# Splitting activations into even and odd halves, and moving side work, in a fused forward and backward kernel of two convolutions and a joint network

## The chip, the cores and the metric

The kernel runs on one core of one Trainium2 chip. The metric is device time in microseconds (us) of one execution. Times are medians of several executions; the span of a profiled execution is some 2 us shorter than its time; it runs from the first instruction to the last.

Engines: PE is TensorE's matmul, PEld its weight load, DVE is VectorE, ACT is ScalarE, POOL is GpSimd, SP is SyncE, which here only issues DMAs. A "q" after an engine means its sequencer, where DMAs are issued. In the code, matmuls write to tiles in PSUM, and copies take their results to SBUF, where `arena` is the kernel's own pool of memory.

## The reference, cut to what matters

```python
B, T, D, K, U = 2, 4000, 512, 15, 8
def _fwd_reference(x, w1, w2, g, w_f, w_g, w_o):
    xp = jnp.pad(x, ((0,0),(pad,pad),(0,0)))
    for i in range(K):  h = h + einsum("btc,cd->btd", xp[:, i:i+T, :], w1[i])
    h = gelu(h)[:, ::2, :]                       # every second row is kept
    ... the same with w2 on h gives f ...         # 1000 rows are left
    fe = einsum("btd,de->bte", f, w_f);  ge = einsum("bud,de->bue", g, w_g)
    j = tanh(fe[:, :, None, :] + ge[:, None, :, :])
    return einsum("btud,dv->btuv", j, w_o)
# the kernel returns this output and the gradients of all seven inputs for a given grad_out
```

All tensors are bf16. Because each convolution keeps every second row, a kernel that wants every second result reads its input with a step of two.

## The kernel before

The kernel has, in order of time: the first convolution, the second one, the joint network with its backward pass block by block, the backward pass of convolution 2 to its input (`acc_bP`, `acc_bQ`, `acc_bR`) and to its weights (`acc_k...`), and the same two for convolution 1. Each convolution is split so that three groups of accumulating matmuls, A, B and C (`acc_l..._0`, `_1`, `_2`), give two rows of results: `A + B` and `B - C`. Inputs are held by parity of the row (`par`), and also as differences of neighbours (`D`).

The forward loop, with the weight sums on POOL and the moving operand that steps by two:

```python
nc.gpsimd.tensor_tensor(WP[:, :, KT:KT + 4, :], WP[:, :, 0:13:4, :], WP[:, :, 2:15:4, :], op=ALU.add)      # L213
nc.gpsimd.tensor_tensor(WP[:, :, KT + 4:KT + 7, :], WP[:, :, 1:10:4, :], WP[:, :, 3:12:4, :], op=ALU.add)  # L214
for wi in range(nwin):
    r0 = wi * win                                        # win = 500
    accs = []
    for li, lst in enumerate(lists):                     # A, B, C
        acc = ps_pool.tile([P, 512], F32, tag="acc", name=f"acc_l{layer}_{li}")
        ...
                a0 = 2 * r0 + off
                nc.tensor.matmul(acc[:, :win], WP[:, cc, wi_, :],
                                 arr[an][:, cc, par, a0:a0 + 2 * win - 1:2], ...)
        accs.append(acc)
    nc.scalar.copy(bs, accs[1][:, :win])
    nc.vector.tensor_tensor(ye, accs[0][:, :win], bs, op=ALU.add)
    nc.vector.tensor_tensor(yo, bs, accs[2][:, :win], op=ALU.subtract)
    emit_out(b, dc, r0, win, ye, yo)                     # two epilogues and the stores
```

Only the B group uses the weight sums.

Start of the kernel: sixteen writes of halo zeros (the padding rows at both ends) to the hidden activations in DRAM are on the SP queue among the x loads.

```python
for b in range(B):
    for dc in range(NC):
        nc.sync.dma_start(HD[:, dc, :, b, 0:HALO], zt[:, :, 0:HALO])
        nc.sync.dma_start(HD[:, dc, :, b, HALO + T2:TH], zt[:, :, 0:HALO])
```

Joint stage: a gradient over 8 values of u is summed on PE with an identity matrix.

```python
pd = pw_f32("pdfe")
for u in range(U):
    nc.tensor.matmul(pd[:, :CH], ident[:], dpre[:, u, :], start=(u == 0), stop=(u == U - 1))
evac("act", DFET[:, ec, b, r0:r0 + CH], pd[:, :CH])
```

End of the joint stage: the w_g gradient leaves PSUM through staging buffers that are released at once, so that the next allocation takes the same place and has to wait for the output write.

```python
for dc in range(NC):
    pwg = pw_f32("pwg")
    nc.tensor.matmul(pwg[:, :D], Gnat[:, dc * P:(dc + 1) * P], DGEN, start=True, stop=True)
    stb, st = AR.new(BF16, [D])
    evac("act", st, pwg[:, :D])
    nc.sync.dma_start(out_6[dc * P:(dc + 1) * P, :], st)
    AR.release(stb)
```

Backward convolution: the order of three groups and the step of two.

```python
for nm in ("P", "Q", "R"):
    ...
        if an == "Y":
            f = 2 * n0 + ofs
            rhs = Y[:, dc, b, f:f + 2 * N + 1:2]
        else:
            rhs = S[:, dc, b, f:f + N + 1]               # always contiguous (all of Q)
        nc.tensor.matmul(acc[:, :N + 1], WT[:, dc, wi_, :], rhs, ...)
```

Last weight gradient: `comp_prep1(1)` starts the load of the even half of x (5.9 MB, on POOL) and then makes differences on VectorE (L1168 before, L1210 after), one for each batch element. One of these has to wait for the last `out_1` writes, whose source it overwrites.

```python
def comp_prep1(comp):
    if comp == 0: ...
    else:
        der["XHe"], der["xhe_blks"] = p5x_load(0, xhe_pre)      # gpsimd DMAs
    ...
    for b in range(B):
        xa, xb, xb2, xc, nr = der[(b, "ops")]
        nc.vector.tensor_tensor(der[(b, "P")], xa, xb, op=ALU.subtract)   # L1168
```

Of the kernel before, what the change touches and what calls it, by code (L numbers as in the profile page):

```python
# [17 lines left out]
P = 128  # L18
# [105 lines left out]
def build_kernel(ctx, tc, x, w1, w2, g, w_f, w_g, w_o, grad_out,  # L124
# [24 lines left out]
    make_identity(nc, ident[:])  # L149

# [22 lines left out]
    def gelu_epilogue(acc, n, tmp, h_out, g_out):  # L173
# [5 lines left out]
        nc.vector.tensor_tensor(h_out, s, acc, op=ALU.mult)  # L179
# [20 lines left out]
    def conv_fwd_k(layer, U_of, D_of, w_dram, n_half, win, emit_out, ps_pool, tmp, wp_blks, after_batch=None, cnt0=0,  # L200
# [4 lines left out]
        for b in range(B):  # L205
            arr = {"U": U_of(b), "D": D_of(b)}
            for dc in range(NC):
# [7 lines left out]
                for wi in range(nwin):  # L215
                    r0 = wi * win
                    accs = []
                    for li, lst in enumerate(lists):
                        acc = ps_pool.tile([P, 512], F32, tag="acc", name=f"acc_l{layer}_{li}")
                        k = 0  # L220
                        nk = NC * len(lst)
                        for cc in range(NC):
                            for (an, par, off, wi_) in lst:
                                a0 = 2 * r0 + off
                                nc.tensor.matmul(acc[:, :win], WP[:, cc, wi_, :],  # L225
                                                 arr[an][:, cc, par, a0:a0 + 2 * win - 1:2],
                                                 start=(k == 0), stop=(k == nk - 1))
                                k += 1
                        accs.append(acc)
# [27 lines left out]
    if "p1" in phases:  # L257
        with ExitStack() as es:
# [17 lines left out]

            for b in range(B):
                nc.gpsimd.memset(XTs[b][:, :, :, 0:HALO], 0.0)
                nc.gpsimd.memset(XTs[b][:, :, :, HALO + T1:TX], 0.0)
            zt = tmp1["hst"]  # L280
            nc.gpsimd.memset(zt[:, :, 0:HALO], 0.0)
            for b in range(B):
                for dc in range(NC):
                    nc.sync.dma_start(HD[:, dc, :, b, 0:HALO], zt[:, :, 0:HALO])
                    nc.sync.dma_start(HD[:, dc, :, b, HALO + T2:TH], zt[:, :, 0:HALO])
# [3 lines left out]
            def prep_x(b):  # L289
                cnt = prep_cnt[0]  # L290
                xb = x[b].rearrange("(blk p par) c -> par p blk c", p=CH, par=2)
                for par in range(2):
                    for gi in range(ngrp):
                        XN = AR.view(xn_blks[cnt % 2], BF16, [gsz, D], parts=CH)
                        dma(nc.sync, XN, xb[par][:, gi * gsz:(gi + 1) * gsz, :])
                        for cc in range(NC):
                            pt = ps_tp.tile([P, 1024], BF16, tag="tp", name="tp_x")
                            for kk in range(gsz):
                                nc.tensor.transpose(pt[:, kk * P:kk * P + CH],
                                                    XN[:, kk, cc * P:(cc + 1) * P], ident[:CH, :CH])  # L300
                            evac("dve" if cc % 2 == 0 else "act",
                                 XTs[b][:, cc, par, HALO + gi * gsz * CH:HALO + (gi + 1) * gsz * CH]
                                 .rearrange("p (k c) -> p k c", c=CH),
                                 pt.rearrange("p (k c) -> p k c", c=P)[:, :gsz, :CH])
                        cnt += 1
                hx = (TX - 1) // 2
                for (k0, k1) in ((0, hx), (hx, TX - 1)):
                    for cc in range(NC):
                        nc.vector.tensor_tensor(DXs[b][:, cc, :, k0:k1], XTs[b][:, cc, :, k0:k1],
                                                XTs[b][:, cc, :, k0 + 1:k1 + 1], op=ALU.subtract)  # L310
# [4 lines left out]
            def emit_out1(b, dc, r0, n, ye, yo):  # L315
                hst, gst = tmp1["hst"], tmp1["gst"]
                gelu_epilogue(ye, n, tmp1, hst[:, 0, :], gst[:, 0:2 * n:2])
                gelu_epilogue(yo, n, tmp1, hst[:, 1, :], gst[:, 1:2 * n:2])
                nc.sync.dma_start(HD[:, dc, :, b, HALO + r0:HALO + r0 + n], hst)
# [4 lines left out]
            def p2_load(b):  # L324
# [8 lines left out]
                for cc in range(NC):  # L333
                    nc.vector.tensor_tensor(dv[:, cc, :, 0:TH - 1], v[:, cc, :, 0:TH - 1], v[:, cc, :, 1:TH],
# [8 lines left out]
            def mid1(b, dc):  # L343
                if b == 0 and dc == 0:
# [13 lines left out]
    def p3_pre(pw_f32, pw_bf16):  # L358
        nc.gpsimd.memset(DFPT[:, :, :, 0:HALO], 0.0)
        nc.gpsimd.memset(DFPT[:, :, :, HALO + T2:TH], 0.0)  # L360
# [121 lines left out]
    def kbwd_accumulate(ps_pool, WT, Y, S, b, n0, N, comp):  # L482
        L = kbwd_lists()
        res = {}
        for nm in ("P", "Q", "R"):
# [4 lines left out]
            for (an, ofs, wi_) in lst:  # L490
                for dc in range(NC):
                    if an == "Y":
                        f = 2 * n0 + ofs
                        rhs = Y[:, dc, b, f:f + 2 * N + 1:2]
# [8 lines left out]
    def p4_setup(pool=None, tag="tp"):  # L503
        blk, DHPT = AR.new(BF16, [NC, B, TX])
        p4_state["DHPT_blk"], p4_state["DHPT"] = blk, DHPT
        nc.gpsimd.memset(DHPT[:, :, :, 0:HALO], 0.0)
        nc.gpsimd.memset(DHPT[:, :, :, HALO + T1:TX], 0.0)
# [71 lines left out]
    if "p3" in phases:  # L579
        with ExitStack() as es:  # L580
# [39 lines left out]
            DPRE = [AR.new(BF16, [U, CH]) for _ in range(NBUF)]  # L620
            JN = [AR.new(BF16, [U, D], parts=CH) for _ in range(NBUF)]
            OST = [AR.new(BF16, [U, D], parts=CH) for _ in range(NBUF)]
            loop_blks = [t[0] for lst in (FE, JT, OMJ, SQT, DO, DOT, DPRE, JN, OST) for t in lst]
# [67 lines left out]
            def emit_dj(k, ecs):  # L691
                b, rr, r0 = sbinfo(k)
                omj, dot = OMJ[k % NBUF][1], DOT[k % NBUF][1]
                for ec in ecs:
# [13 lines left out]
                    pd = pw_f32("pdfe")  # L708
                    for u in range(U):
                        nc.tensor.matmul(pd[:, :CH], ident[:], dpre[:, u, :], start=(u == 0), stop=(u == U - 1))  # L710
                    evac("act", DFET[:, ec, b, r0:r0 + CH], pd[:, :CH])
# [8 lines left out]
            def emit_batch_end(b):  # L720
                g2blk, G2T = AR.new(BF16, [NC, T2])
                nc.sync.dma_start(G2T, G2D[b])
                for dc in range(NC):
                    for wi in range(T2 // W2N):
                        s0 = wi * W2N
                        pf = pw_f32("pdf")
                        for ec in range(NC):
                            nc.tensor.matmul(pf[:, :W2N], WFT[:, ec, dc * P:(dc + 1) * P], DFET[:, ec, b, s0:s0 + W2N],
                                             start=(ec == 0), stop=(ec == NC - 1))
                        nc.vector.tensor_tensor(DFPT[:, dc, b, HALO + s0:HALO + s0 + W2N], pf[:, :W2N],  # L730
                                                G2T[:, dc, s0:s0 + W2N], op=ALU.mult)
# [27 lines left out]
            if "p4" in phases:  # L759
                blk, SQ2 = AR.new(BF16, [NC, B, T2 // 2 + 4])  # L760
                SQ2_st["blk"], SQ2_st["v"] = blk, SQ2
                k = 0
                for b in range(B):
                    for dc in range(NC):
                        eng = nc.vector if k % 2 == 0 else nc.gpsimd
                        eng.tensor_tensor(SQ2[:, dc, b, :], DFPT[:, dc, b, 0:TH - 1:2], DFPT[:, dc, b, 1:TH:2],
# [491 lines left out]
```

## Time and profile before

| | before |
|---|---|
| median time | 2190.79 us (4 runs, 2189.94 to 2193.62) |
| span of the profiled run | 2186.3 us |
| PE busy | 2061.4 us, 94% |
| PE idle inside its span (from the gaps between matmuls) | 113.3 us |
| half clock granted to PE (from the clock records) | 68.3 us, PE busy in 27.7 us of them |

PE is the limit, so two things count: how long each matmul occupies PE, and where PE idles. An idle gap of a few us can also bring a stretch at half clock that outlasts it. The Trainium skill (TensorE: Matmul & The Clock Gate, "Part 1: The HAM clock gate") describes this with windows of about 3.4 us; the trace agrees, its half-clock stretches are 3.41, 6.83, 10.24, 13.65 and 30.7 us long.

The groups of PE instructions of the kernel before, shapes kept apart. The columns are line, engine, operation, output and input, shapes and count, then busy us and the mean ns of one, then the idle time of PE just before them and who ended it.

```profile
L225 PE MATMUL acc_l<-arena 128*128 128x500 bf16 x2208 | 497.8, 386 | 3.5 <-POOL arena L213 2.3 <-POOL arena L214 0.9 <-DMA arena<-in_w_dram 0.3
L498 PE MATMUL acc_bP<-arena 128*128 128x501 bf16 x768 | 183.9, 383 | 0.7 <-ACT arena L166 0.7
L498 PE MATMUL acc_bQ<-arena 128*128 128x501 bf16 x768 | 174.1, 375 | 0.0
```

The mean of one runs from issue to the modelled end, and successive matmuls overlap, so it is not what one costs. The cost is the time from one start to the next, which I took from the trace at full clock: 222 ns for `acc_l`, `acc_bP` and `acc_bR` (median), 212 for `acc_bQ`, 210 for `pj`. The mean of `acc_l` is 223.6. The means above show the same difference: 386 and 383 for the operands with a step, 375 for `acc_bQ`, which is contiguous.

The waits of PE in the kernel before (engine, what waited, for what; total us, times, longest):

```profile
PE acc_kP L843 <- DVE arena L1168: 22.6, 1, 22.6
...
PE tp_dfp L930 <- ACT arena L166: 14.1, 3, 12.6
...
PE tpdo L666 <- DMA arena<-in_grad_out_dram: 8.3, 1, 8.3
PE tp_dx L1116 <- DVE arena L1066: 7.7, 3, 3.8
...
PE pge L416 <- DVE arena L168: 1.5, 1, 1.5
...
PE pdf L728 <- DVE arena L730: 1.2, 1, 1.2
```

Not shown are, among others, 17.6 us in four waits for the x loads. The largest of the list, in order of time (start, duration, engine, line, operation; in brackets the idle time before it and who ended it). Several other instructions lie between these lines.

```profile
1837.84 1.36 POOL L544 DMA_DIRECT2D arena<-in_x_dram  x1
...
1843.76 0.62 SPq L159 DMA_DIRECT2D out_dram<-arena  x1
...
1862.96 3.09 DVE L1168 TENSOR_TENSOR arena<-arena 125x5632 bf16<-125x5632 bf16 x1 [18.69 <-DMA out_dram<-arena]
1866.11 2.31 PE L843 MATMUL acc_kP<-arena 125*128 125x512 bf16 x5 [22.57 <-DVE arena L1168]
```

Read it backwards. PE waits for the VectorE subtraction, which waits for the out_dram writes issued from 1843.76 on. That wait ends at 1862.96 only, 19.2 us after the first of these writes was issued, with the 5.9 MB x load under way, which was issued just before them, from 1837.84 on.

### The profile page before, as it was taken

How to read it: one execution, taken by the hardware profiler on the slowest of the kernel's cores; microseconds unless marked ns; L12 is line 12 of the kernel's file. 1: busy time of each engine (PE TensorE's matmuls, PEld its weight loads, DVE VectorE, ACT ScalarE, POOL GpSimd, SP SyncE). 2: the span in 40 equal slices, each digit the busy share in tenths (PEclk: the TensorE clock that was granted, in tenths of full speed). 3: DMA queues.
4: the chain of work that ended last, by engine and by line, in shares of the span. 5: the costliest groups of instructions: out<-in, count | busy, mean ns of one | idle time of the engine just before them, and what ended most of it. 6: DMA issues, size and time to landing. Idle time of an engine off the chain costs nothing.

```text
span 2186.3 us, 29569 instructions
## 1 busy us (share of the span) xinstructions
PE 2061.4 (94%) x12032; PEld 1050.7 (48%) x12032; DVE 847.4 (39%) x1970; ACT 570.4 (26%) x1143; POOL 484.5 (22%) x424
## 2 busy tenths in 40 slices
PE   5999999999899999999799998899999996899999
PEld 3444444444566656666444444444445443344444
DVE  2554433543555555556364533432322232111310
ACT  1322122121655545552311233311212331000000
POOL 1332322353544444453020010130100001000000
PEclk9999999999999999999899999999999998899999
DMA  9423424653222222224310022134210104100000
GB/s 176 102 65 82 112 65 109 154 108 66 90 76 76 77 77 76 76 76 139 132 37 1 20 92 73 51 104 83 59 26 20 29 19 101 45 27 26 25 25 25
DMA packets 227408, 154.14 MB, mean 71 GB/s; under 512 B 167728, under 2 KB 219348, under 8 KB 223016
## 3 DMA queue, kind: packets, MB, share of 16 engines
q1 hardware_dynamic: 203592, 119.99, 21.0%
q10 hardware_dynamic: 19392, 20.49, 3.3%
q0 software_dynamic: 4288, 11.78, 2.5%
q8 instruction: 94, 1.54, 0.3%
q14 instruction: 42, 0.34, 0.1%
HBM read 100.02 MB, written 52.17 MB: 70 GB/s over the span
## 4 chain that ended last, share of the span: by engine, by line
PE 45%; ACT 3%; DVE 2%; DMA 1%; issue 1%; ACTq 0%; POOL 0%; DVEq 0%
PE acc_bP L498 7%; PE acc_bQ L498 7%; PE acc_kP L843 7%; PE acc_kR L843 7%; PE acc_bR L498 6%; PE acc_kQ L843 6%; ACT arena L166 2%; PE acc_k L866 2%; PE tp_wk L476 1%; DMA out_dram<-arena 1%; PE tp_dx L1116 1%; PE tp_hnk L1007 1%; DVE arena L168 0%; PE tp_dhp L1083 0%; DVE arena L1064 0%
## 5 line engine op out<-in xcount | busy, mean ns | idle before, releaser
L225 PE MATMUL acc_l<-arena 128*128 128x500 bf16 x2208 | 497.8, 386 | 3.5 <-POOL arena L213 2.3
L225 PEld LDWEIGHTS <-arena 128*128 128x128 bf16 x2208 | 212.8, 97 | 283.1 <-issue 5.8
L498 PEld LDWEIGHTS <-arena 128*128 128x128 bf16 x2208 | 211.4, 97 | 253.5 <-issue 1.0
L843 PEld LDWEIGHTS <-arena 125*128 125x128 bf16 x2016 | 196.6, 98 | 255.9 <-DVE arena L1168 22.8
L498 PE MATMUL acc_bP<-arena 128*128 128x501 bf16 x768 | 183.9, 383 | 0.7 <-ACT arena L166 0.7
L843 PE MATMUL acc_kP<-arena 125*128 125x512 bf16 x672 | 158.1, 383 | 22.6 <-DVE arena L1168 22.6
L658 POOL TENSOR_TENSOR arena<-arena 128x500 f32<-128x500 bf16 x128 | 130.4, 1019 | 202.7 <-ACT arena L650 202.6
L498 PE MATMUL acc_bQ<-arena 128*128 128x501 bf16 x768 | 174.1, 375 | 0.0
L650 ACT ACTIVATE arena<-arena 128x125 bf16<-128x125 f32 x512 | 158.7, 398 | 55.2 <-DVE arena L168 55.2
L498 PE MATMUL acc_bR<-arena 128*128 128x501 bf16 x672 | 158.6, 384 | 0.0
L843 PE MATMUL acc_kQ<-arena 125*128 125x512 bf16 x672 | 156.5, 379 | 0.0
L704 DVE SCALAR_TENSOR_TENSOR arena<-arena,pj 128x125 bf16<-128x125 bf16 x512 | 111.7, 282 | 112.6 <-PE pj L699 112.4
L843 PE MATMUL acc_kR<-arena 125*128 125x512 bf16 x672 | 155.0, 379 | 0.0
L717 PE MATMUL gwo<-arena 125*128 125x512 bf16 x512 | 141.6, 379 | 0.0
L848 ACT COPY arena<-acc_kQ 128x512 f32<-128x512 f32 x56 | 32.8, 586 | 399.3 <-PE acc_kQ L843 383.3
L850 DVE TENSOR_TENSOR arena<-acc_kP,arena 128x512 bf16<-128x512 f32 x56 | 38.7, 691 | 222.9 <-PE acc_kP L843 219.3
L699 PE MATMUL pj<-arena 128*128 128x500 bf16 x512 | 118.4, 373 | 5.4 <-ACT arena L166 5.3
L181 POOL TENSOR_TENSOR arena<-arena 128x500 f32<-128x500 f32 x48 | 63.1, 1315 | 241.8 <-ACT arena L178 230.9
L675 PE MATMUL po<-arena 128*125 128x512 bf16 x512 | 113.3, 379 | 0.0
L1064 DVE TENSOR_TENSOR arena<-arena 128x500 bf16<-128x500 f32 x32 | 23.8, 745 | 202.5 <-ACT arena L1062 202.5
L213 POOL TENSOR_TENSOR arena<-arena 128x2048 bf16<-128x2048 bf16 x16 | 65.4, 4088 | 116.0 <-DMA arena<-in_w_dram 116.0
L232 DVE TENSOR_TENSOR arena<-acc_l,arena 128x500 f32<-128x500 f32 x24 | 16.3, 678 | 190.1 <-ACT arena L231 190.1
(136 smaller groups left out, 2187.4 us busy)
## 6 DMA issues: line engine op xcount, KB each, us to landing
arena<-in_w_dram SPq DMA_DIRECT2D x64, 480.0 KB
out_dram<-arena SPq DMA_DIRECT2D x132, 128.0 KB
arena<-in_w_dram SPq DMA_DIRECT2D x8, 1920.0 KB
arena<-in_grad_out_dram SPq DMA_DIRECT2D x16, 896.0 KB
out_dram<-arena ACTq DMA_DIRECT2D x16, 896.0 KB
arena<-in_x_dram POOLq DMA_DIRECT2D x4, 2576.0 KB, 23.1
arena<-in_x_dram SPq DMA_DIRECT2D x8, 896.0 KB
arena<-HD SPq DMA_DIRECT2D x2, 2016.0 KB
```

The source lines that it names most:

```text
L166: nc.scalar.copy(out_ap, in_ap)
L181: nc.gpsimd.tensor_tensor(xsq, sm, z, op=ALU.mult)
L213: nc.gpsimd.tensor_tensor(WP[:, :, KT:KT + 4, :], WP[:, :, 0:13:4, :], WP[:, :, 2:15:4, :], op=ALU.add)
L225: nc.tensor.matmul(acc[:, :win], WP[:, cc, wi_, :], arr[an][:, cc, par, a0:a0 + 2 * win - 1:2], start=(k == 0), stop=(k == nk - 1))
L498: nc.tensor.matmul(acc[:, :N + 1], WT[:, dc, wi_, :], rhs, start=(k == 0), stop=(k == nk - 1))
L650: nc.scalar.activation(jt[:, ec, u, :], fe[:, ec, :], ACT.Tanh, bias=GE[:, ec, b * U + u:b * U + u + 1])
L658: nc.gpsimd.tensor_tensor(sq, jt[:, :, u, :], jt[:, :, u, :], op=ALU.mult)
L675: nc.tensor.matmul(po[:CH, :D], jt[:, ec, u, :], WO[:, ec, :], start=(ec == 0), stop=(ec == NC - 1))
L699: nc.tensor.matmul(pj[:, :4 * CH], WOT[:, vc, ec * P:(ec + 1) * P], dot[:, vc, 4 * uh:4 * uh + 4, :].rearrange("p u r -> p (u r)"), start= ...
L704: nc.vector.scalar_tensor_tensor(dpre[:, u, :], omj[:, ec, u, :], 1.0, pj[:, ul * CH:(ul + 1) * CH], op0=ALU.mult, op1=ALU.mult, accum_out ...
L717: nc.tensor.matmul(GWO[ec][:, :D], jn[:, u, ec * P:(ec + 1) * P], do[:, u, :], start=(k == 0 and u == 0), stop=(k == nsb_tot - 1 and u == ...
L843: nc.tensor.matmul(acc[:, :D], data(b, comp, kind, l + m, cc), dy(b, dk, l), start=(k == 0), stop=(k == nk - 1))
```

## The change

The intent: (1) hold each activation as an even and an odd half, so that a step of two becomes contiguous; (2) take a quarter of the `pdfe` sums from PE to VectorE; (3) start sooner, with the halo writes later and the groups in the order A, C, B, because only B needs the weight sums; (4) in the last stage hold the x load back behind a subtraction, by a tiny POOL copy into its target (the gate); (5) backward groups in the order P, R, Q, so that less is left after the last group; (6) smaller de-interleaving copies shared by ACT and VectorE. Core of the diff; the rest follows the new layout.

```diff
-                    accs = []
-                    for li, lst in enumerate(lists):
+                    accs = [None, None, None]
+                    for li in (0, 2, 1):
+                        lst = lists[li]
...
                                 a0 = 2 * r0 + off
+                                m0 = (a0 % 2) * (arr[an].shape[-1] // 2) + a0 // 2
                                 nc.tensor.matmul(acc[:, :win], WP[:, cc, wi_, :],
-                                                 arr[an][:, cc, par, a0:a0 + 2 * win - 1:2],
+                                                 arr[an][:, cc, par, m0:m0 + win],
...
-            for b in range(B):
-                for dc in range(NC):
-                    nc.sync.dma_start(HD[:, dc, :, b, 0:HALO], zt[:, :, 0:HALO])
-                    nc.sync.dma_start(HD[:, dc, :, b, HALO + T2:TH], zt[:, :, 0:HALO])
+            def halo_zeros():
+                HDz = HD.rearrange("p c r b t -> p (c r b) t")
+                nc.sync.dma_start(HDz[:, :, 0:HALO // 2], zt[:, :, 0:HALO // 2])
+                nc.sync.dma_start(HDz[:, :, HH - HALO // 2:HH + HALO // 2], zt)
+                nc.sync.dma_start(HDz[:, :, TH - HALO // 2:TH], zt[:, :, 0:HALO // 2])
...
             def mid1(b, dc):
+                if b == 0 and dc == 1:
+                    halo_zeros()
...
-        for nm in ("P", "Q", "R"):
+        for nm in ("P", "R", "Q"):
...
-                        rhs = Y[:, dc, b, f:f + 2 * N + 1:2]
+                        m0 = (f % 2) * (Y.shape[-1] // 2) + f // 2
+                        rhs = Y[:, dc, b, m0:m0 + N + 1]
...
+                    if ec % 4 == 3 and U == 8:
+                        tr = TRS[k % NBUF][1]
+                        df = dpre.rearrange("p u r -> p (u r)")
+                        nc.vector.tensor_tensor(tr[:, 0:4 * CH], df[:, 0:4 * CH], df[:, 4 * CH:8 * CH], op=ALU.add)
+                        nc.vector.tensor_tensor(tr[:, 4 * CH:6 * CH], tr[:, 0:2 * CH], tr[:, 2 * CH:4 * CH], op=ALU.add)
+                        nc.vector.tensor_tensor(DFET[:, ec, b, r0:r0 + CH], tr[:, 4 * CH:5 * CH], tr[:, 5 * CH:6 * CH],
+                                                op=ALU.add)
+                    else:
...
-                else:
-                    der["XHe"], der["xhe_blks"] = p5x_load(0, xhe_pre)
...
                     nc.vector.tensor_tensor(der[(b, "P")], xa, xb, op=ALU.subtract)
+                if comp == 1:
+                    for b in range(B):
+                        nc.gpsimd.tensor_copy(AR.view(xhe_pre[b], BF16, [L1 + 7, D], parts=CH)[:, 0, 0:1],
+                                              der[(B - 1, "P")][:, 0, 0:1])
+                    der["XHe"], der["xhe_blks"] = p5x_load(0, xhe_pre)
```

## The prediction

> **What bounds the kernel.** TensorE. The page gives PE 94% of 2186 us, DVE 39%, ACT 26%, POOL 22%; the table by stage shows PE busy 322 of 325 us in the first convolution, 165 of 165 in the second, 439 of 444 in the joint stage, 317 of 320 in the last weight gradient. Starts of successive matmuls (trace, full clock) separate two rates. The Trainium skill (TensorE: Matmul & The Clock Gate, Back-to-back issue gap) gives N/2.4 + 2.5 ns: 211 for N=500. `pj` (500 contiguous columns) takes 210 and `acc_bQ` (501 contiguous, at odd and even offsets) 212: they agree. But `acc_l`, `acc_bP` and `acc_bR`, whose moving operand steps by two bf16, take 222 (`acc_l` mean 223.6). The skill (SBUF — State Buffer, note on cachelines) would have that stride free, with several hits per 16-byte line; the trace says about 11 ns each.
>
> **What the change does.**
> 1. It stores each activation as an even and an odd half, so these operands become contiguous: 2208 `acc_l` matmuls save about 12 ns (-26 us), 1440 `acc_bP`/`acc_bR` save 10 ns (-14 us). All on PE, which is critical in those stages.
> 2. A quarter of the `pdfe` identity-matmul sums (128 of 512, about 58 ns each) go to three VectorE adds per block. DVE is half idle there: -6 us.
> 3. Start: sixteen tiny halo writes sat on the SP queue between the halves of the second x load (issued 1.8 and 15.5 us); PE waited 6.1 us for it. They move later. The order A, C, B needs POOL's weight sums last: the waits of 2.3 and 0.9 us and the half-clock window at 44.5 to 51.3 us should go. Together -10 us.
> 4. Last stage: PE idles 22.6 us before the first `acc_kP`, for a DVE subtraction that waits for out_dram writes, which land late among the x load issued on POOL just before (DMA 90% busy, mostly the software queue). The load now waits for that subtraction: the writes should land in 2 to 4 us (estimate), leaving about 9 us idle: -13 us.
> 5. P, R, Q order: after the last group of a pass only one DVE operation is left instead of an ACT copy and three; the `tp_dx` waits of 2.0, 1.8, 3.8 us shrink: -5 us.
> 6. De-interleaving copies are halved and shared by ACT (2.0 us per 1008 elements now) and DVE; derivative writes step 2 instead of 4 (1.5 to 1.6 us each now). Mostly hidden: -3 us.
> 7. Added: four HD writes per window instead of one, two half-size multiplies instead of one at each batch end, SQ2 on DVE alone. About +2 us.
>
> The 12.6 us idle before `tp_dfp` (PSUM held by the last `pwg` copies, whose staging waits for output writes) and the 8.3 us before `tpdo` should stay.
>
> **Prediction.** Sum -75 us: 2116 us, range 2098 to 2134. Faster by over 2%: 0.95; within 2%: 0.05; slower: 0.00.
>
> **What would show it.** Start-to-start of `acc_l`, `acc_bP`, `acc_bR` at 210 to 213 ns; first convolution matmul about 5 us earlier, no POOL wait; idle before `acc_kP` near 9 us; joint stage about 7 us shorter, nothing new waiting for the VectorE sums.
>
> **What would make it wrong.** The extra 11 ns may not come from the stride; the epilogue, serial through single buffers, may not keep up with faster windows; the thousands of 4 and 8 byte halo writes may delay weight loads; out_dram writes may land late for another reason.

## More of the kernel before

The epilogue of one half window ends with a POOL multiply and a VectorE operation with two SBUF inputs (L182 before, L187 after), here called the last epilogue step:

```python
def gelu_epilogue(acc, n, tmp, h_out, g_out):
    ...
    nc.gpsimd.tensor_tensor(xsq, sm, z, op=ALU.mult)
    nc.vector.scalar_tensor_tensor(g_out, xsq, 1.0, s, op0=ALU.add, op1=ALU.mult)     # L182
```

## The result, and the profile after

| | before | after |
|---|---|---|
| median time | 2190.65 us (12 runs, 2189.32 to 2194.03) | 2128.91 us (8 runs, 2124.36 to 2137.27) |
| ratio of the fast runs | | 0.9718, 95% interval 0.9705 to 0.973 |
| span of the profiled run | 2186.3 us | 2122.6 us |
| PE busy / idle inside its span | 2061.4 / 113.3 us | 2023.3 / 87.7 us |
| half clock, and PE busy in it | 68.3, 27.7 us | 64.9, 38.0 us |

A ratio is the mean time of one kernel's fast runs over that of the other's in the same rounds, so it is not quite the ratio of the medians. Executions over 1.5% slower than the fastest of the same kernel are left out of the means. The change is faster by 2.8%, inside the predicted range, but it saves 62 us where 75 were predicted. The sections that follow ask where the 13 us went. The runs of the changed kernel also spread over 13 us, those of the kernel before over 5; the profiled one is the fastest of the eight.

The stages tell more than the sum. Each is the time from one event on PE to the next, read from the trace. The two columns on the right belong to experiments that are told below.

| stage, from the event above to this one | before | after | difference | sums on VectorE | all edits |
|---|---|---|---|---|---|
| first `acc_l` (from the start) | 33.2 | 28.6 | -4.6 | 28.8 | 28.6 |
| last transpose of x | 74.3 | 71.3 | -3.0 | 70.4 | 61.8 |
| first `tpw` (rest of convolution 1) | 272.9 | 259.8 | -13.2 | 259.8 | 259.8 |
| first `acc_l` of convolution 2 | 6.0 | 13.8 | **+7.8** | 10.0 | 10.0 |
| first `pfe` (convolution 2) | 165.8 | 160.4 | -5.4 | 160.2 | 160.0 |
| first `po` | 14.3 | 7.6 | -6.8 | 7.6 | 7.6 |
| first `pdf` of batch element 2 (joint stage) | 443.7 | 435.4 | -8.4 | 435.1 | 435.0 |
| first `tpf` | 14.4 | 17.8 | **+3.5** | 14.4 | 14.6 |
| first `acc_bP` | 44.0 | 44.4 | +0.4 | 45.8 | 32.2 |
| first `tp_hnk` | 185.3 | 180.5 | -4.8 | 179.9 | 182.1 |
| first `acc_bP` of convolution 1 | 211.3 | 212.5 | **+1.2** | 208.9 | 209.2 |
| first `tp_dhp` | 275.3 | 266.5 | -8.8 | 262.5 | 262.7 |
| first `acc_kQ` of the last stage | 93.7 | 93.1 | -0.6 | 93.1 | 93.0 |
| first `acc_kP` of the last stage | 32.0 | 11.6 | -20.4 | 11.6 | 11.6 |
| end of the span | 320.2 | 319.4 | -0.8 | 319.2 | 319.3 |

The groups of PE instructions after, as before:

```profile
L232 PE MATMUL acc_l<-arena 128*128 128x500 bf16 x2208 | 473.3, 376 | 0.9 <-DVE arena L323 0.9
L522 PE MATMUL acc_bP<-arena 128*128 128x501 bf16 x768 | 179.6, 378 | 0.7 <-ACT arena L167 0.7
```

From start to start `acc_l` now takes 211 ns, `acc_bP` and `acc_bR` 212. The rates are those predicted, and the wait for POOL's weight sums before `acc_l` is gone.

The waits of PE after:

```profile
PE tp_dfp L968 <- ACT arena L167: 14.1, 1, 14.1
PE pge L439 <- DVE arena L169: 8.7, 1, 8.7
PE acc_kP L876 <- DVE arena L1210: 7.0, 1, 7.0
...
PE tp_hnk L1047 <- DVE arena L169: 4.5, 2, 3.8
...
PE pdf L762 <- DVE arena L739: 3.7, 1, 3.7
```

The wait before `acc_kP` fell from 22.6 to 7.0 us, and that for `grad_out` before `tpdo` is gone, which I had said would stay. Three waits are new or much longer: `pge` 1.5 to 8.7, `pdf` 1.2 to 3.7, `tp_hnk` with a longest of 3.8. All three wait for VectorE. VectorE in order of time in the changed kernel, at the end of convolution 1 and before the last `pdf` group:

```profile
363.00 0.71 DVE L187 SCALAR_TENSOR_TENSOR arena<-arena 128x500 bf16<-128x500 f32 x1 [0.80 <-POOL arena L186]
...
367.71 4.54 DVE L187 SCALAR_TENSOR_TENSOR arena<-arena 128x500 bf16<-128x500 f32 x1 [0.80 <-POOL arena L186]
...
978.44 3.84 DVE L739 TENSOR_TENSOR arena<-arena 128x125 bf16<-128x125 f32 x1
```

POOL at the same times:

```profile
367.64 4.04 POOL L218 TENSOR_TENSOR arena<-arena 128x2048 bf16<-128x2048 bf16 x1
...
978.09 4.05 POOL L487 TENSOR_TENSOR arena<-arena 128x2048 bf16<-128x2048 bf16 x1 [3.16 <-PE pdf L762]
```

The same VectorE operation takes 0.71 us once and 4.54 us the next time. The second time it began 0.07 us after a POOL weight sum and ended 0.6 us after it. The copies that PE needs for `pge`, 0.9 us of work, stand behind it in VectorE's queue. The other two waits look the same. L739, the last VectorE add of a sum, takes 3.84 us (median 0.28) beside the weight sum L487. A copy before `tp_hnk` takes 4.30 us beside the next one:

```profile
1227.87 4.05 POOL L487 TENSOR_TENSOR arena<-arena 128x2048 bf16<-128x2048 bf16 x1 [7.28 <-DMA arena<-in_w_dram]
1227.89 4.30 DVE L169 COPY arena<-arena 128x504 bf16<-128x504 bf16 x1 [1.43 <-PE tp_hnk L1047]
```

That suggested a theory, which the experiments below test: VectorE stands still while such a sum runs on POOL.

The last stage after, in order of time:

```profile
1797.86 0.30 POOL L1213 COPY arena<-arena 125x1 bf16<-125x1 bf16 x2 [5.29 <-DVE arena L1210]
...
1798.66 1.38 POOL L569 DMA_DIRECT2D arena<-in_x_dram  x1
...
1800.02 3.09 DVE L1210 TENSOR_TENSOR arena<-arena 125x5632 bf16<-125x5632 bf16 x1 [1.63 <-DMA out_dram<-arena]
```

The gate copy (POOL L1213) was released by the first subtraction (1794.71 to 1797.79), which waits for no write. It is the second one, at 1800.02, that waits for the writes. So the load was not held behind that one, as I had predicted; it started 1.4 us before it. But the first writes had been issued at 1796.60, ahead of the load, and PE went on with `acc_kP` at 1803.17.

### The profile page after: what moved, and what is told of

Its sections match the earlier page's. It is cut to its first block, busy times and chain, and to the rows that moved or that the text cites. A ratio compares the mean times of both kernels' runs of the same rounds, so it can differ in the third digit from the quotient of the medians.

```text
span 2122.6 us, 29361 instructions
## 1 busy us (share of the span) xinstructions
PE 2023.3 (95%) x11904; PEld 1052.9 (50%) x11904; DVE 878.3 (41%) x2062; ACT 558.0 (26%) x1143; POOL 482.6 (23%) x430
## 4 chain that ended last, share of the span: by engine, by line
PE 85%; ACT 8%; DVE 3%; DMA 2%; issue 1%; ACTq 0%; POOL 0%; SPq 0%; DVEq 0%; POOLq 0%
PE acc_l L232 22%; PE acc_bP L522 7%; PE acc_bQ L522 7%; PE acc_kP L876 7%; PE acc_kR L876 7%; PE acc_kQ L876 7%; PE acc_bR L522 6%; PE pj L725 5%; PE gwo L751 5%; ACT arena L167 4%; ACT arena L676 3%; PE acc_k L899 2%; PE tp_wk L499 2%; PE po L701 1%; PE tpdo L692 1%
## 5 line engine op out<-in xcount | busy, mean ns | idle before, releaser
L232 PE MATMUL acc_l<-arena 128*128 128x500 bf16 x2208 | 473.3, 376 | 0.9 <-DVE arena L323 0.9
L232 PEld LDWEIGHTS <-arena 128*128 128x128 bf16 x2208 | 215.5, 98 | 252.9 <-issue 5.4
L522 PEld LDWEIGHTS <-arena 128*128 128x128 bf16 x2208 | 213.6, 98 | 239.0 <-issue 2.5
L522 PE MATMUL acc_bP<-arena 128*128 128x501 bf16 x768 | 179.6, 378 | 0.7 <-ACT arena L167 0.7
L522 PE MATMUL acc_bR<-arena 128*128 128x501 bf16 x672 | 153.9, 376 | 0.0
L751 PE MATMUL gwo<-arena 125*128 125x512 bf16 x512 | 137.1, 379 | 0.0
L187 DVE SCALAR_TENSOR_TENSOR arena<-arena 128x500 bf16<-128x500 f32 x48 | 78.5, 1634 | 53.1 <-POOL arena L186 53.1
L487 POOL TENSOR_TENSOR arena<-arena 128x2048 bf16<-128x2048 bf16 x8 | 33.3, 4164 | 254.4 <-DMA arena<-in_w_dram 200.0
```

Source lines behind the costliest of these rows:

```text
L232: nc.tensor.matmul(acc[:, :win], WP[:, cc, wi_, :], arr[an][:, cc, par, m0:m0 + win], start=(k == 0), stop=(k == nk - 1))
L522: nc.tensor.matmul(acc[:, :N + 1], WT[:, dc, wi_, :], rhs, start=(k == 0), stop=(k == nk - 1))
L751: nc.tensor.matmul(GWO[ec][:, :D], jn[:, u, ec * P:(ec + 1) * P], do[:, u, :], start=(k == 0 and u == 0), stop=(k == nsb_tot - 1 and u == ...
```

## The experiments

Twelve kernels ran. The changed kernel did not run beside them; differences are taken to its median of 2128.91 us, and the kernel before had medians of 2190.6 to 2192.0 us.

### The layout alone

The kernel before with only the operand's step taken away, nothing stored differently. It reads wrong elements; shapes, waits and counts are those of before.

```diff
-                                                 arr[an][:, cc, par, a0:a0 + 2 * win - 1:2],
+                                                 arr[an][:, cc, par, a0:a0 + win],
...
-                        rhs = Y[:, dc, b, f:f + 2 * N + 1:2]
+                        rhs = Y[:, dc, b, f:f + N + 1]
```

> The kernel before, with only the step of the moving operand taken away in the forward and backward convolutions (the same start, columns next to each other, so results are wrong on purpose; nothing else moves). Theory, the step of two costs the 11 ns: starts of acc_l, acc_bP and acc_bR fall from 222 to 211 or 212 ns, and the time falls by 2208 x 12 + 1440 x 10 = 41 us, to about 2150 us, without any change of layout. Rival, the 11 ns belong to these matmuls for another reason (weights, accumulation): they stay at 222 ns and the time stays at 2190 us.

Measured: 2159.17 us, ratio 0.9851 (0.9831 to 0.9871), so 31 us of median and 27.3 us of span. The start-to-start times fell to 211 and 212 ns. Without the waits in it the mean of `acc_l` fell from 222.2 to 211.4 ns, so multiplied by the counts the rates alone would give 38 us (2208 × 10.8 + 1440 × 10.1 ns); the 41 us expected took the waits for a part of the rate. Most of the rest is found on PE: it idles 3.5 us more (116.8), and its busy time at half clock rose from 27.7 to 40.5 us; half of these 12.8 us, 6.4 us, is lost. My reading, which no run tests, is that the side chains were not made faster, so a faster PE meets them sooner, and short waits tip it into half-clock stretches. The mechanism holds; the gain on the clock is about three quarters of the product.

### What a step costs

The changed kernel, with convolution 1 reading its operand in steps of 1, 2, 4 and 8 for its four output blocks. Its output is wrong, which doesn't matter for the time.

```diff
+                                rhs = arr[an][:, cc, par, m0:m0 + win]
+                                if layer == 1:
+                                    sp = (1, 2, 4, 8)[dc]
+                                    rhs = arr["U"][:, cc].rearrange("p r t -> p (r t)")[:, off:off + sp * (win - 1) + 1:sp]
```

> The changed kernel, with the moving operand of the first convolution read at steps of 1, 2, 4 and 8 elements for the four output blocks dc 0 to 3 (wrong results on purpose). Theory, [...]211 ns at step 1, 222 at step 2, and clearly more at 4 and again at 8[...]. Rival, any step other than 1 costs a fixed 11 ns: 222 at 2, 4 and 8.

Measured (a single look, of unknown state; start to start at full clock): 211, 222, 442 and 879 ns. The cost is not a fixed 11 ns. From a step of 2 on it follows the span of memory that the 500 elements of one partition cover: 2000 bytes in 222 ns, 4000 in 442, 8000 in 879, which is 9.0 to 9.1 bytes per ns each time. At that rate the 1000 bytes of step 1 would take 111 ns (an estimate from these numbers), well under the 211 measured. The figure for a step of 8 rests on seven pairs at full clock. In most of those blocks PE was granted half the clock (163.8 and 177.5 us in one piece) although its matmuls followed each other without a gap, and there they also started 879 ns apart (median of 358 pairs). At this step the clock did not set the pace. A step of two lies just beyond the break-even point: 222 against 211. This is why the change gains only 5% on these matmuls. The Trainium skill (SBUF — State Buffer, "Door 1: The DMA port swizzle", note on cachelines) would have bf16 stride free up to 8; for a matmul's moving operand the measurement contradicts it.

### The gate

The changed kernel with the x load back where it was.

```diff
+                else:
+                    der["XHe"], der["xhe_blks"] = p5x_load(0, xhe_pre)
...
-                if comp == 1:
-                    for b in range(B):
-                        nc.gpsimd.tensor_copy(...der[(B - 1, "P")][:, 0, 0:1])
-                    der["XHe"], der["xhe_blks"] = p5x_load(0, xhe_pre)
```

> The changed kernel with the x load of the last stage put back where it was (issued before the subtraction, without the POOL copies that hold it back). Theory: out_dram writes again land late behind the load, PE again idles about 22 us before the first acc_kP instead of 7, and the time rises by 15 to 20 us. Rival, the shorter idle comes from the P, R, Q order (the last transposes start sooner): the idle stays under 10 us and the time within 3 us.

Measured: 2148.52 us, ratio 0.9805 (0.9787 to 0.9823), 20 us above the changed kernel; in its trace the stage before `acc_kP` is 15.6 us longer. The idle before `acc_kP` is back at 22.6 us; the load was issued from 1797.9 on, the writes from 1806.3 on, and they landed at 1825.3. The gate is needed.

### The order P, Q, R

The changed kernel with the backward groups in the old order.

```diff
-        for nm in ("P", "R", "Q"):
+        for nm in ("P", "Q", "R"):
```

> The changed kernel with the backward groups in the old order P, Q, R. Theory: the waits of tp_dx at the ends of passes return (0.2 us in the changed kernel's last pass, 1.8 to 3.8 us before) and the idle before acc_kP is about the same: 3 to 6 us slower. Rival, the order matters little: within 2 us.

Measured: 2144.79 us, ratio 0.9788 (0.9772 to 0.9804): 16 us above the changed kernel, not a few. The gate is still there, and the idle before `acc_kP` is 22.3 us all the same. Its last stage in order of time:

```profile
1802.36 3.08 DVE L1210 TENSOR_TENSOR arena<-arena 125x5632 bf16<-125x5632 bf16 x1
1805.37 0.67 DVE L1106 TENSOR_TENSOR arena<-acc_bQ,arena 128x500 bf16<-128x500 f32 x1
...
1806.61 1.39 POOL L569 DMA_DIRECT2D arena<-in_x_dram  x1
...
1807.84 0.61 SPq L160 DMA_DIRECT2D out_dram<-arena  x1
...
1826.37 3.09 DVE L1210 TENSOR_TENSOR arena<-arena 125x5632 bf16<-125x5632 bf16 x1 [18.41 <-DMA out_dram<-arena]
```

In this order the first subtraction comes before L1106, the last operation that the out_1 writes need. So the gate opens before the writes are issued, and the load goes ahead of them by 1.2 us. In the changed kernel L1106 comes before the first subtraction. The gain of the last stage therefore came from gate and order together; each alone gives nothing there.

### The order P, Q, R with the gate on both batch elements

If only the place of the load counts, a gate on both subtractions must bring the gain back without the new order.

```diff
-                        nc.gpsimd.tensor_copy(AR.view(xhe_pre[b], ...)[:, 0, 0:1],
-                                              der[(B - 1, "P")][:, 0, 0:1])
+                        for b2 in range(B):
+                            nc.gpsimd.tensor_copy(AR.view(xhe_pre[b], ...)[:, 0, b2:b2 + 1],
+                                                  der[(b2, "P")][:, 0, 0:1])
```

(and the order as in the run before)

> The changed kernel with P, Q, R in the backward pass (as the earlier run that lost 16 us) and the gate on the subtractions of both batches, so that the x load is issued after the one that waits for the out_dram writes. Theory (the order mattered through the place of the load against those writes): the idle before the first acc_kP falls from 22.3 to 8 to 10 us, and the time is about 13 us below the run with P, Q, R and the single gate: 2131. Rival (the order P, Q, R costs by itself, by the longer tail after the last pass): idle stays above 18 us and the time at 2142 to 2147.

Measured: 2121.87 us, ratio 0.9692 (0.9671 to 0.9712), 23 us below the run before. The idle is 7.1 us:

```profile
1795.22 3.09 DVE L1210 TENSOR_TENSOR arena<-arena 125x5632 bf16<-125x5632 bf16 x1 [3.17 <-DMA out_dram<-arena]
1798.37 1.89 PE L876 MATMUL acc_kP<-arena 125*128 125x512 bf16 x4 [7.05 <-DVE arena L1210]
...
1798.95 1.37 POOL L569 DMA_DIRECT2D arena<-in_x_dram  x1 [0.26 <-POOL arena L1214]
```

The wait for the writes ends 3.5 us after the first of them was issued (at 1791.73), as in the changed kernel (3.4 us), where it took 18.5 us in the run before, 19.0 without the gate and 19.2 in the kernel before. The load starts afterwards, when nothing waits for it. This settles the cause of the idle time. I had expected 13 us of gain; 23 came. The two profiled runs are even 30.6 us apart. Of these, 15.0 are the last stage; 8.3 are the transposes of x in the first stage (79.5 against 71.2 us) and 6.5 the stage of `tp_hnk`. The code is the same in these two, so they vary from run to run; why is said at the end of the account below.

This run is also no slower than the changed kernel with its P, R, Q. By stage, P, R, Q gains 3.4 us in the backward pass of convolution 1 and 4.3 before `acc_kP`, and loses 3.9 us up to the first `tp_hnk` and 1.5 between the first `tp_dhp` and the last stage (both runs with P, Q, R agree within 0.3 us on the three of these that the gate does not touch). At `tp_hnk` the cause shows in the trace: the copies on ACT and VectorE (L167, L169) that feed it are released by the last `acc_bQ` matmul, and in the new order that one comes a group later. Order P, R, Q helps one tail and hurts another; about 2 us are left.

### The sums on PE again

The changed kernel with all `pdfe` sums on PE.

```diff
-                    if ec % 4 == 3 and U == 8:
+                    if ec % 4 == 5 and U == 8:
```

> The changed kernel with every pdfe sum back on TensorE (no VectorE sums). Theory: the two stretches of the joint stage, 215.7 and 219.6 us in the changed kernel, grow by about 3.5 us each (64 matmuls of 58 ns), while the 3.7 us wait of pdf for the last VectorE add (3.84 us instead of 0.5, as POOL's weight sum runs beside it) goes away with its half-clock window: net 1 to 5 us slower, so near 2131 us. Rival, VectorE's extra work also slows the blocks: the stage does not grow, and the time falls by some 4 us.

Measured: 2136.5 us (2130.23 to 2145.25), ratio 0.9754 (0.9726 to 0.9783), 8 us above the changed kernel, where 1 to 5 were expected. Its runs overlap those of the changed kernel; the stages say more. The two halves of the joint stage are 5.7 and 5.9 us longer, more than the 3.7 each that 64 matmuls of 58 ns give. The rest is a wait: `pj` waits 5.0 us in total (13 times) for ACT's copies out of PSUM, 0.2 us in the changed kernel. Each sum on VectorE also saves ACT a copy. The wait before the last `pdf` group (the product of the summed gradient with w_f) gave 3.3 us back. So the item is worth 8 us net, and the wait that it adds comes from its last add, L739: 3.84 us instead of the median 0.28, beside POOL's weight sum L487.

### The forward order A, B, C

The changed kernel with the forward groups in the old order.

```diff
-                    for li in (0, 2, 1):
+                    for li in (0, 1, 2):
```

> The changed kernel with the forward groups in the old order A, B, C. Theory: in the first window PE waits for POOL's weight sums again (about 3 us, and a half-clock window of some 3 us loss), so 3 to 7 us more. Rival, the earlier loads alone removed that wait: no wait for POOL, time within 2 us. The 9 us idle in front of pge, which I hold to come from a collision of POOL's weight sums with a VectorE operation, may come or go with this order.

Measured: 2117.2 us (2116.99 to 2118.53), ratio 0.9663 (0.9645 to 0.9682): 12 us faster than the changed kernel, where I had expected it slower. So the new order is a loss in this kernel. The two profiled executions differ by 6.0 us only (2122.6 and 2116.6), as that of the changed kernel was its fastest, so the traces show half of the gain. Three effects, from the traces:

- The stage from `tpw` to convolution 2 takes 5.0 us instead of 13.8. In the order A, C, B both epilogues wait for the last group, B; in A, B, C one of them begins a group earlier. Besides, the last epilogue step is over 4 us long 1 time in 48, 11 times in the changed kernel and 1 in the kernel before: the later epilogue falls on POOL's sums for the next block of output channels.
- The 8.3 us wait for `grad_out` before `tpdo` is back, and its stage is 5.9 us longer. The first half of the joint stage is 4.2 us shorter in exchange (211.5 against 215.7): 2.6 us of waits of `po` for VectorE's copies are gone, and 0.8 us lost to half clock. The wait for `grad_out` comes from the place of a write on the SP queue. In A, B, C the second part of the load stands behind the write of the last epilogue's result. SP in order of time, with the order A, B, C and then in the changed kernel:

```profile
532.05 0.33 SPq L461 DMA_DIRECT2D G2D<-arena  x1
532.43 0.40 SPq L161 DMA_DIRECT2D arena<-in_grad_out_dram  x1
```

```profile
525.16 0.33 SPq L160 DMA_DIRECT2D arena<-in_grad_out_dram  x1
525.55 0.39 SPq L161 DMA_DIRECT2D arena<-in_grad_out_dram  x1
...
546.32 0.34 SPq L461 DMA_DIRECT2D G2D<-arena  x1
```

- The first windows wait again, but for VectorE's differences (L323), not for POOL: 6.6 us in three waits. One of these differences took 4.94 us instead of 1.2, beside a POOL weight sum.

### The transposes' copies on ACT

The changed kernel with the copies of the transposed joint weights on ACT, so that they do not stand behind VectorE's long step.

```diff
-                    evac("dve", dst[:, nc_, k0 * P:(k0 + kn) * P], pt[:, :kn * P])
+                    evac("act", dst[:, nc_, k0 * P:(k0 + kn) * P], pt[:, :kn * P])
...
-        evac("dve", GT, ...)
+        evac("act", GT, ...)
```

> The changed kernel with the copies of the transposed w_f, w_o and g out of PSUM on ScalarE instead of VectorE. Theory: pge waits 8.7 us only because these copies queue behind one VectorE operation that POOL's weight sum holds up for 4.5 us; on ScalarE they pass it, the wait falls to 1 or 2 us, and the half-clock window after it shrinks: 6 to 9 us less, near 2121 us. Rival, something else on the way (the g load, PSUM buffers) sets the wait: it stays near 8 us.

Measured: 2122.85 us (2114.92 to 2129.22), ratio 0.9687 (0.9661 to 0.9714). The wait before `pge` falls to 4.6 us and its stage from 13.8 to 8.3 us. The expected 1 or 2 us were missed: the queue behind the long step was not the only cause, and the test of the theory below leaves about the same rest. The time is 6 us lower, but the runs spread over 14 us. The stage is the evidence, not the time.

### The halo writes later

The changed kernel with the halo writes one block of output channels (`dc`) later; their zeros are made from that block's own result, so that the writes can't be issued sooner.

```diff
-            nc.gpsimd.memset(zpool_t[:, :], 0.0)
             def halo_zeros():
+                nc.vector.tensor_scalar(zpool_t[:, :], tmp1["gst"][:, 0:NC * 2 * B * 4], 0.0, 0.0, op0=ALU.mult, op1=ALU.add)
...
-                if b == 0 and dc == 1:
+                if b == 0 and dc == 2:
```

> The changed kernel with the three halo writes made to wait for a later window (the zeros are made from a staging tile written about 150 us in), out of the way of the second batch's x loads. Theory: the third and fourth x load are issued some 5 us earlier, the 5.4 us wait of tp_x and the half-clock window at 85 us go: 5 to 9 us less, near 2121 us. Rival, the x loads are late for other reasons (buffers of the transposes, four HD writes per window): the wait stays above 4 us.

Measured: 2121.72 us (2120.57 to 2123.22), ratio 0.9684 (0.967 to 0.9699), 7 us faster. In the changed kernel the three writes (from 60.49 on, 5.5 us of issue; the last is shown) and the weights keep SP busy until the next x load is issued at 76.81:

```profile
65.08 0.99 SPq L296 DMA_DIRECT2D HD<-zeros  x1
66.18 10.54 SPq L215 DMA_DIRECT2D arena<-in_w_dram  x3
76.81 3.06 SPq L160 DMA_DIRECT2D arena<-in_x_dram  x1
```

PE waits for that load at 81.7 us and is granted half the clock from 85.6 to 92.4 us:

```profile
87.14 1.86 PE L313 MATMUL tp_x<-ident,arena 125*128 125x125 bf16 x16 [5.40 <-DMA arena<-in_x_dram]
```

With the edit this wait is gone and the stage takes 66.5 us instead of 71.3. The change had moved the halo writes from one pair of x loads to in front of the next.

### The weight sums on VectorE

This is the test of the theory: the changed kernel with the weight sums moved from POOL to VectorE, forward and backward. VectorE gets more work, but nothing large runs beside it on POOL.

```diff
-                nc.gpsimd.tensor_tensor(WP[:, :, KT:KT + 4, :], ...)
-                nc.gpsimd.tensor_tensor(WP[:, :, KT + 4:KT + 7, :], ...)
+                nc.vector.tensor_tensor(WP[:, :, KT:KT + 4, :], ...)
+                nc.vector.tensor_tensor(WP[:, :, KT + 4:KT + 7, :], ...)
...
-        nc.gpsimd.tensor_tensor(WN[:, KT:KT + 4, :], ...)
-        nc.gpsimd.tensor_tensor(WN[:, KT + 4:KT + 7, :], ...)
+        nc.vector.tensor_tensor(WN[:, KT:KT + 4, :], ...)
+        nc.vector.tensor_tensor(WN[:, KT + 4:KT + 7, :], ...)
```

> The changed kernel with the weight sums (both layers and the backward ones) on VectorE instead of POOL. Theory (VectorE instructions with two SBUF inputs stretch from 0.7 to about 4.5 us when a POOL weight sum runs beside them, and what queues behind them makes PE wait): the slow ones among the 48 runs of the second multiply of the gate derivative fall from 13 to 0 or 2, the weight-transpose wait of 8.7 us in the second convolution to about 1.5 us, the waits of 3.7 us before the first w_f gradient and before the first hidden-activation transpose go, the first-window stage is no longer spread. Time 2110 to 2118. Rival (the waits come from the order A, C, B and from thin slack, not from the two engines colliding): the waits stay near their size, or the sums block VectorE's queue until the weights land, and the time stays at 2125 or rises.

Measured: 2111.62 us (2108.93 to 2112.56), ratio 0.9636 (0.9622 to 0.9651), 17 us faster than the changed kernel. VectorE at the end of convolution 1:

```profile
367.03 0.71 DVE L187 SCALAR_TENSOR_TENSOR arena<-arena 128x500 bf16<-128x500 f32 x1 [0.79 <-POOL arena L186]
...
368.40 1.22 DVE L218 TENSOR_TENSOR arena<-arena 128x2048 bf16<-128x2048 bf16 x1
```

The step is 0.71 us again, and the sum itself takes 1.22 us here instead of 4.04 on POOL. Of the 48 last epilogue steps two are 1.5 us long and none longer (in the changed kernel two of 1.5 and eleven of 4.5). VectorE's busy time fell from 878.3 to 845.2 us although it got 48 more operations; POOL's fell from 482.6 to 304.1. The waits of PE:

```profile
PE pge L439 <- DVE arena L169: 4.9, 1, 4.9
...
PE tp_hnk L1047 <- DVE arena L169: 1.0, 1, 1.0
...
PE pdf L762 <- DVE arena L739: 0.8, 1, 0.8
```

The wait before `pdf` fell from 3.7 to 0.8 us, the longest waits for VectorE's copies before `tp_hnk` from 3.8 to 1.0 (that for L1033, 4.0 us, stays), and the runs spread over 4 us instead of 13. The theory holds in all these. It missed in one: the wait before `pge` is 4.9 us, not 1.5. That rest fits the order A, C, B, which leaves both epilogues to the end: the copies still stand behind the last epilogue step in VectorE's queue. With A, B, C (and POOL's sums) the wait is 1.5; the two edits were not run together.

### Three edits, and a fourth

The first kernel has the sums on VectorE, the halo writes later, and the gate on both batch elements, with P, R, Q and A, C, B kept.

> The changed kernel with three edits: weight sums on VectorE, halo writes made one window later with zeros that depend on it, gate on both batches. If the effects add: about 10 to 14 us from the sums, 5 to 7 from the halo writes, about 0 from the gate (P, R, Q already has the load behind the writes): 2105 to 2112. If the VectorE sums only shift the waits: 2118 to 2122, as the halo run alone.

Measured: 2103.16 us (2101.61 to 2104.28), ratio 0.9599 (0.9585 to 0.9613), 26 us below the changed kernel. The gains add: 17 from the sums, 7 from the halo writes, which makes 24.

The second one adds separate staging for the w_g gradient.

```diff
+            pwg_st = []
             for dc in range(NC):
                 ...
-                AR.release(stb)
+                pwg_st.append(stb)
+            for stb in pwg_st:
+                AR.release(stb)
```

> The run before, and the staging of the last w_g-gradient copies not reused within the loop, so that the PSUM banks which the first grad-activation transposes wait for (14 us in the changed kernel) come free without waiting for output writes. Theory: that wait falls to about 2 us, and the time is 10 to 12 us below the run before: about 2096. Rival (another wait, the de-interleaving copies, ends as late): 2105 to 2110.

Measured: 2089.26 us (2088.43 to 2089.49), ratio 0.9535 (0.9519 to 0.9551), with correct results; 13.9 us below the run before. The PE wait before `tp_dfp`, 14.3 us in the run before:

```profile
PE tp_dfp L971 <- ACT arena L167: 2.1, 1, 2.1
```

That stage, up to the first `acc_bP`, fell from 46.3 (the run before) to 32.2 us. This is the fastest version: 4.6% below the kernel before, where the change had 2.8%. PE idles 60.4 us in its span, against 87.7 in the changed kernel, and is at half clock for 37.5 us, against 64.9.

## Why the prediction was right or wrong

The total was inside the range. Term by term:

| term of the prediction | predicted | shown |
|---|---|---|
| 1 contiguous operands | -40 | rates nearly as predicted (-38 by rate × count), alone worth -27 of span, -31 of median |
| 2 sums to VectorE | -6 | -11.5 in the joint stage, +3.3 in a new wait: -8 |
| 3 start | -10 | first `acc_l` -4.6 as named; the next stage -3.0, of which 254 faster matmuls give 2.7 (10.8 ns each), so next to nothing from the rest |
| 3 order A, C, B, elsewhere | not seen | +8.8 before `pge`, -5.9 before `po` (each against the order A, B, C) |
| 4 last stage | -13 | idle -15.6; size right, mechanism wrong |
| 5 P, R, Q | -5 | `tp_dx` waits 7.7 to 2.7 us as predicted; most of it given back before `tp_hnk` and around `tp_dhp` |
| 6, 7 copies, additions | -1 | not separated |
| `tp_dfp` stays, `tpdo` stays | 0 | `tp_dfp` 12.6 to 14.1; `tpdo` gone (-8.3) |

**Right: what bounds the kernel, and what the layout does to each matmul.** The start-to-start times fell as said, and the run with only the step taken away shows them without the rest. Mis-sized: the step "-26 and -14 us, all on PE, which is critical in those stages". Multiplying a rate by a count took all other chains to be out of the way. In the run of the layout alone about 6.4 us of it went to half-clock time and 3.5 to new idle. The 12 ns for `acc_l` also came from a mean with the first window's waits in it; 10.8 ns is its rate, and the other 3 us were booked a second time in term 3.

**Right in size, wrong in mechanism: the last stage.** The failed step is "The load now waits for that subtraction". The gate reads the other subtraction, which waits for no write. What put the writes in front of the load was the gate together with P, R, Q. The run with P, Q, R and the gate kept (22.3 us idle) and the one with a gate on both (7.1 us) show it. It also means that terms 4 and 5 were not independent; adding them was right by luck.

**Wrong: term 3.** The failed step is "They move later", with the gain of the start booked in full. The halo writes moved in front of another x load, and PE waits 5.4 us for that one and runs at half clock after it. The first part, the earlier first matmul and the end of POOL's wait, came as named (no wait for POOL came back with A, B, C either, so it is not shown that the order ended it). Its other failed step is "The order A, C, B needs POOL's weight sums last", taken as a gain only: it also puts both epilogues after the last group.

**Missed: VectorE and POOL take turns.** Nothing in the prediction compared what runs on these two engines at one time. In the kernel before the collision was there, one last epilogue step in 48; the new order moved it under eleven, and the last VectorE add of term 2 under another weight sum. "Nothing new waiting for the VectorE sums" failed by this. The Trainium skill (SBUF — State Buffer, "Who interferes with whom") states it: a VectorE instruction with two SBUF inputs contends with a GpSimd instruction that reads SBUF, and the second one blocks fully. The trace agrees (0.72 us becomes 4.5, the length of the POOL sum and a little more), and also for a copy with one input (0.4 becomes 4.3 us), where the page names the two-port modes of copies. Copies from PSUM beside such a sum kept their length (two took 0.73 us from 372.15 on, while L219 ran). I read that page before the prediction only for its note on strides. Moving the sums away gives back 17 us, more than the missing 13.

**Missed in my favour:** the `grad_out` load, whose place on the SP queue depends on when the last epilogue's write can go, and the ACT copies saved in the joint stage (5 us of `pj` waits).

**From run to run: the same collision.** The stage that begins with `tp_hnk` takes 206.7 to 220.0 us in the profiled runs of kernels that are alike there but for the backward order and have the sums on POOL. It follows one wait, that of `tp_hnk` for VectorE's copies (L169): 0 us in the shortest, 4.5 in the changed kernel (212.5), 9.0 in the longest, the run without the gate. In these traces copies of 0.4 us last 2.7 to 4.3 us beside the sums L487 and L488, and where the sums fall on them differs. With the sums on VectorE the wait is 0.9 to 1.0 us and the stage 208.9 to 210.0 in all three kernels.

What stays open: how much of terms 6 and 7 is real, and whether A, C, B is still a loss with the sums on VectorE, which was not run against A, B, C. The spread of the changed kernel's runs fits this collision and the one in its first windows (VectorE differences of 1.2 us become 4 to 5 us when the first weight sum overlaps them, in some profiled runs and not in others), and it shrinks with the sums on VectorE, but only one run of each kernel was profiled.

## What to carry to other kernels

Before you shift work or reorder groups in a tuned kernel, list what the other engines and the DMA queues do in the same microseconds: a change of order moves the tails, and what counts is which queue entry ends up ahead of which. When one of two engines that block each other, here POOL and VectorE, has a long operation, price moving it to the faster one first: the sum took a third of the time there and stopped blocking its neighbour. Treat rate × count as an upper bound, and test a gain that needs two edits with each one alone.

## What the Trainium skill lacked or had wrong

- SBUF — State Buffer, "Door 1", note on cachelines: it gives a free stride of up to 8 bf16. For a matmul's moving operand of 500 bf16 the time from start to start was 211, 222, 442 and 879 ns at steps 1, 2, 4 and 8, that is 9.0 to 9.1 bytes of span per ns and partition beyond a step of 1 (one run).
- TensorE: Matmul & The Clock Gate, "Back-to-back issue gap": it calls N/2.4 + 2.5 ns the isolated gap and gives about 131 ns per matmul of N=512 as the sustained rate with weight loads. Here each matmul has its own weight load in long streams, and N=512 took 216 ns, N=500 210 to 211, N=501 212: the formula holds for the sustained rate too.
- GPSIMD Engine Reference, "3.1 Elementwise — side-by-side cycle accounting": it gives a ratio of 1.96 for an f32 add, and none for bf16. In bf16 with 128x2048 elements the add took 4.06 us on POOL and 1.21 us on VectorE, a ratio of 3.4.
- SBUF — State Buffer, "Who interferes with whom": right, and its "DVE 6.8× slower" is near the 6.3 times found here (0.72 us became 4.5, eleven times in 48). It lacks what this costs others: before what stood behind such an instruction in VectorE's queue PE waited up to 8.7 us.
- DMA: Bandwidth & Descriptors, "Issuing engines are not separate DMA queues": it says that DMAs of all queues interleave, but has no price for small writes behind a large load on another queue. Issued 1.2 us after the start of a 5.9 MB load they kept their reader waiting until 18.5 us after the first of them was issued; issued ahead of the load, 3.4 us.
